# An attention and MLP kernel on one core: quad 0 turned at full width, its loads reordered, one A@V evacuated by two engines

## The chip, the cores and the metric

The kernel runs on 1 core of one Trainium2 chip. The metric is the device time of one execution in microseconds (us). An experiment gives several timed executions, each with the core's span and its mean granted TensorE clock, and one profile of one execution. All executions here count as "fast" (none is 1.5% above the fastest of its kernel).

Engines: PE is the TensorE matmul, PEld its weight load, DVE is VectorE, ACT ScalarE, POOL GpSimd, SP SyncE. The granted clock is the share of TensorE's full clock that the trace records; below, "warm" is the full clock (1.00 in the traces) and "cold" half of it (0.50).

## The reference

```python
# q, k, v: (8, 12, 448, 64) fp32; then an MLP over 3584 tokens, 768 -> 2048 -> 768
scores = np.matmul(q, k.transpose(0, 1, 3, 2)) / np.sqrt(64)
attn   = np.maximum(scores, 0.0) ** 2 / 448
x      = np.matmul(attn, v)                      # (..) -> (3584, 768)
h      = x @ w_in
g      = np.maximum(h, 0.0) + alpha * np.minimum(h, 0.0)
out    = g @ w_out
```

## The kernel before

Heads are handled four at a time, in a "quad"; there are 24 quads, three per batch. For each quad q and k are cast to bf16, turned (transposed) and multiplied; the scores get relu and square on ACT and DVE, then A@V follows and its result is scaled into `xT`, the MLP's input. Quad 0 is loaded as fp32 and cast on chip; quads 1 to 5 come by casting transfers that GpSimd issues. To keep these from taking bandwidth from quad 0, GpSimd first waits for the small load of alpha. The code is shortened; `...` and comments stand for what is left out.

```python
nc.scalar.dma_start(out=alpha_sb, in_=moe_alpha...)          # ahead of all
nc.sync.dma_start(out=raw[(0, "q")]..., in_=flat(0, "q"))
for js in (first, rest):
    nc.sync.dma_start(out=raw[(0, "k")][:, :, lo:hi]..., in_=...)
make_identity(nc, ident); make_identity(nc, ident_f)
cast[(1, "k")] = early_pool.tile([128, 2, NJ, D], BF16, tag="k", name="ke")
nc.gpsimd.tensor_copy(cast[(1, "k")][:KF, 0, 0, 0:1], alpha_sb[:, 0:1])   # the wait
nc.gpsimd.dma_start(out=cast[(1, "k")]..., in_=flat(1, "k"))
load_bf16(1, "q"); load_bf16(0, "v"); load_bf16(1, "v")
warm(15)                                    # dummy matmuls
nc.vector.tensor_copy(cast[(0, "q")][:, 0], raw[(0, "q")][:, 0])
nc.scalar.copy(cast[(0, "q")][:, 1], raw[(0, "q")][:, 1])
transpose(0, "q")
# ... k likewise, then scores(0, 0..2); the loop over quads 0 to 2:
            if j == 3 and not last:
                transpose(n + 1, "k")
            if j == 4 and not last:          # after this step's squares
                transpose(n + 1, "q")
                squares(keep=1)
# ... the turn itself, two 64-column matmuls for each j:
        for j in js:
            for s in range(2):
                nc.tensor.transpose(ps[64 * s:64 * s + 64, j], t[:, s, j], ident)
# ... the last A@V of batch 1 and its neighbours:
    ffn1(1, 0, range(0, 4)); ffn1(1, 1, range(0, 4))
    attnv(5)                                 # one tile, one ACT evacuation of 896
    feed(7, "v")()
    ffn1(1, 2, range(0, 4))
    for ff in range(3):
        ffn1(1, ff, range(4, KM))            # needs attnv(5)'s result
```

## Time and profile before

| | us |
|---|---|
| median of the first 3 executions | 391.43 |
| span of the profiled one | 390.1 |
| raw q of quad 0 lands | 4.61 |
| first scores | 6.66 |
| first MLP matmul | 22.22 |
| from there to the end | 367.86 |

The last four rows are read from starts and landings in the trace. They cut the span into four pieces, landing of q, landing to first scores, first scores to first MLP matmul, and the rest. The lines themselves stand in the prediction.

### The profile page before, as it was taken

What the parts mean: (1) busy time and instruction counts of PE and PEld (TensorE: products, weight loads), DVE (VectorE), ACT (ScalarE), POOL (GpSimd) and SP (SyncE); (2) the same over time, 40 slices, a digit from 0 to 9 for tenths busy, and PEclk for the clock granted to TensorE, in tenths of its full rate; (3) what the DMA queues carried; (4) which work ended last, traced back from release to release, by engine and by line L of the source; (5) the groups of instructions that cost most, each with busy time, mean ns of one, the idle gap of its engine ahead of it and who ended that gap; (6) DMA issues with size and microseconds to landing.
All of it is one profiled execution on the core that took longest, in us unless ns stands there. A gap on an engine that the chain in (4) does not pass through costs nothing.

```text
span 390.1 us, 7871 instructions
## 1 busy us (share of the span) xinstructions
PE 379.2 (97%) x3210; PEld 215.0 (55%) x3210; DVE 252.1 (65%) x335; ACT 215.6 (55%) x361; POOL 73.3 (19%) x88
## 2 busy tenths in 40 slices
PE   7699999999999999999999999999999999999996
PEld 4345556445665456645665456654566545655564
DVE  3976877587677757766674666777676376725411
ACT  5975767574556656654474645766565365624200
POOL 5664000061241014201231012311030000000000
PEclk9999999999999999999999999999999999999999
DMA  7999997893995528926494354947163220130033
GB/s 155 185 208 205 203 221 271 239 319 83 237 271 184 114 76 232 229 64 165 87 276 141 66 164 96 247 159 172 30 91 85 72 47 2 42 81 2 0 82 81
DMA packets 64755, 55.43 MB, mean 142 GB/s; under 512 B 35776, under 2 KB 60496, under 8 KB 64720
## 3 DMA queue, kind: packets, MB, share of 16 engines
q1 hardware_dynamic: 53472, 44.77, 44.2%
q0 software_dynamic: 10976, 9.96, 16.1%
q8 instruction: 25, 0.41, 0.4%
q10 hardware_dynamic: 272, 0.21, 0.2%
q14 instruction: 10, 0.08, 0.1%
HBM read 45.62 MB, written 11.01 MB: 145 GB/s over the span
## 4 chain that ended last, share of the span: by engine, by line
PE 94%; DMA 3%; ACT 1%; DVE 1%; issue 0%
PE hps L255 37%; PE ops L271 37%; PE avh L223 7%; PE sc L156 6%; PE sch L156 3%; DMA ke<-in_k_dram 2%; PE ops L294 1%; PE tps L131 1%; PE av L223 1%; DMA qraw<-in_q_dram 1%; ACT rl L185 1%; ACT xT L241 0%; DVE gT L263 0%; ACT rl L163 0%; DVE rl L165 0%
## 5 line engine op out<-in xcount | busy, mean ns | idle before, releaser
L255 PE MATMUL hps<-xT,w_in_sb 128*128 128x448 bf16 x768 | 149.3, 353 | 0.8 <-ACT xT L232 0.4
L271 PE MATMUL ops<-w_out_sb,gT 128*128 128x384 bf16 x864 | 145.8, 326 | 0.0
L263 DVE SCALAR_TENSOR_TENSOR gT<-neg,beta_sb,hps 128x448 bf16<-128x448 f32 x128 | 85.7, 679 | 61.1 <-ACT neg L262 60.2
L271 PEld LDWEIGHTS <-gT 128*128 128x128 bf16 x864 | 83.4, 98 | 61.2 <-issue 7.9
L255 PEld LDWEIGHTS <-w_in_sb 128*128 128x128 bf16 x768 | 74.0, 98 | 72.8 <-issue 5.9
L262 ACT ACTIVATE neg<-hps 128x448 f32<-128x448 f32 x128 | 69.0, 545 | 63.8 <-PE hps L255 63.7
L185 ACT ACTIVATE rl<-sc 128x896 bf16<-128x896 f32 x87 | 77.1, 923 | 44.4 <-PE sc L156 44.3
L196 DVE TENSOR_TENSOR at<-rl 128x1792 bf16<-128x1792 bf16 x80 | 85.5, 1112 | 2.1 <-ACT rl L185 0.9
L106 DVE COPY osb<-ops 128x384 f32<-128x384 f32 x30 | 16.7, 557 | 46.0 <-PE ops L271 46.0
L163 ACT ACTIVATE rl<-sch 128x448 bf16<-128x448 f32 x81 | 41.6, 550 | 4.6 <-PE sch L156 4.6
L106 POOL CAST kb<-kraw 128x896 bf16<-128x896 f32 x16 | 18.4, 1152 | 115.2 <-DMA kT<-kb 55.7
L156 PE MATMUL sc<-qT,kT 64*64 64x448 bf16 x456 | 35.9, 355 | 3.8 <-ACT rl L185 1.5
L223 PE MATMUL avh<-at,vb 64*64 64x448 bf16 x588 | 34.2, 350 | 0.0
L156 PEld LDWEIGHTS <-kT 64*64 64x64 bf16 x672 | 21.9, 106 | 20.1 <-issue 13.0
L104 ACT COPY osb<-ops 128x384 f32<-128x384 f32 x24 | 11.4, 475 | 36.0 <-PE ops L271 36.0
L223 PEld LDWEIGHTS <-vb 64*64 64x64 bf16 x672 | 25.6, 106 | 9.3 <-issue 4.9
L183 DVE TENSOR_SCALAR rl<-sc 128x896 bf16<-128x896 f32 x27 | 29.4, 1090 | 0.6 <-PE sc L156 0.6
L106 POOL CAST vb<-vraw 128x896 bf16<-128x896 f32 x16 | 16.8, 1050 | 36.5 <-PE avh L223 36.0
L156 PE MATMUL sch<-qT,kT 64*64 64x448 bf16 x216 | 22.5, 355 | 0.0
L106 POOL CAST qb<-qraw 128x896 bf16<-128x896 f32 x16 | 15.9, 991 | 32.3 <-DMA qT<-qb 32.3
L165 DVE TENSOR_SCALAR rl<-sch 128x448 bf16<-128x448 f32 x27 | 16.8, 622 | 2.6 <-ACT xT L239 0.8
L238 DVE TENSOR_SCALAR xT<-avh 128x448 bf16<-128x448 f32 x19 | 11.9, 625 | 7.7 <-PE avh L223 7.7
(55 smaller groups left out, 96.8 us busy)
## 6 DMA issues: line engine op xcount, KB each, us to landing
out_dram<-osb SPq DMA_DIRECT2D x54, 192.0 KB, 2.7
qraw<-in_q_dram SPq DMA_DIRECT2D x19, 448.0 KB, 5.4
kraw<-in_k_dram SPq DMA_DIRECT2D x18, 448.0 KB, 4.4
vraw<-in_v_dram SPq DMA_DIRECT2D x18, 448.0 KB, 6.3
w_out_sb<-in_moe_w_out_dram POOLq DMA_DIRECT2D x2, 1536.0 KB, 20.0
w_in_sb<-in_moe_w_in_dram POOLq DMA_DIRECT2D x8, 192.0 KB, 8.3
w_in_sb<-in_moe_w_in_dram POOLq DMA_DIRECT2D x4, 384.0 KB, 9.7
vb<-in_v_dram POOLq DMA_DIRECT2D x6, 224.0 KB, 9.7
```

Of the source, the lines that this page charges most:

```text
L106: eng.tensor_copy(o, i)
L156: nc.tensor.matmul(half[r][64 * c:64 * c + 64, :S], kT[n][64 * r:64 * r + 64, j, c, :], qT[n][64 * r:64 * r + 64, :, c, :], start=True, st ...
L163: nc.scalar.activation(rl[:, r], half[r][:, :S], ACTF.Relu)
L165: nc.vector.tensor_scalar(rl[:, r], half[r][:, :S], 0.0, None, ALU.max)
L183: nc.vector.tensor_scalar(rl, ps[:, :, :S], 0.0, None, ALU.max)
L185: nc.scalar.activation(rl, ps[:, :, :S], ACTF.Relu)
L196: nc.vector.tensor_tensor(a, t, t, ALU.mult)
L223: nc.tensor.matmul(half[r][64 * s:64 * s + 64, :S], vb[n][64 * r:64 * r + 64, s, j, :], a[64 * r:64 * r + 64, s], start=(j == 0), stop=(j ...
L255: nc.tensor.matmul(ps, w_in_sb[:, km // 2, km % 2, bass.ts(ff, 128)], xT[b][:, km // 2, km % 2, :], start=(km == 0), stop=(km == KM - 1))
L262: nc.scalar.activation(neg, ps, ACTF.Relu, scale=-1.0)
L263: nc.vector.scalar_tensor_tensor(gT[b // 2][:, ff, (b % 2) * S:(b % 2) * S + S], neg, beta_sb[:, ff:ff + 1], ps, ALU.mult, ALU.add)
L271: nc.tensor.matmul(ps, gT[sb][:, ff, bass.ts(c, 128)], w_out_sb[:, ff, bass.ts(hf, 384)], start=(ff == 0), stop=(ff == KF - 1))
```

## The change

It is meant to shorten the opening: fewer transposes for quad 0, nothing ahead of its load, casting transfers that start after a fixed delay instead of after alpha. One more edit lets two engines evacuate the last A@V of batch 1 side by side. A piece of dead code goes as well (not shown).

```diff
+        if n == 0:
+            t = t.rearrange("p j s d -> p j (s d)")
...
         for j in js:
+            if n == 0:
+                nc.tensor.transpose(ps[:, j], t[:, j], ident)
+                continue
             for s in range(2):
...
-    nc.scalar.dma_start(out=alpha_sb, in_=moe_alpha.rearrange("(kf p) -> kf p", p=128))
-        cast[(0, w)] = early_pool.tile([128, 2, NJ, D], BF16, tag=w, name=f"{w}e")
+        cast[(0, w)] = early_pool.tile([128, NJ, 2, D], BF16, tag=w, name=f"{w}e")
...                                          # after the three loads of quad 0:
+    nc.sync.dma_start(out=alpha_sb, in_=moe_alpha.rearrange("(kf p) -> kf p", p=128))
-    cast[(1, "k")] = early_pool.tile([128, 2, NJ, D], BF16, tag="k", name="ke")
-    nc.gpsimd.tensor_copy(cast[(1, "k")][:KF, 0, 0, 0:1], alpha_sb[:, 0:1])
-    nc.gpsimd.dma_start(out=cast[(1, "k")]..., in_=flat(1, "k"))
-    load_bf16(1, "q")
+    for w in "qk":
+        cast[(1, w)] = early_pool.tile([128, 2, NJ, D], BF16, tag=w, name=f"{w}e")
+        nc.gpsimd.memset(cast[(1, w)], 0.0)
+    for w in "kq":
+        nc.gpsimd.dma_start(out=cast[(1, w)]..., in_=flat(1, w))
-    nc.vector.tensor_copy(cast[(0, "q")][:, 0], raw[(0, "q")][:, 0])
-    nc.scalar.copy(cast[(0, "q")][:, 1], raw[(0, "q")][:, 1])
+    nc.vector.tensor_copy(cast[(0, "q")][:, :, 0], raw[(0, "q")][:, 0])
+    nc.scalar.copy(cast[(0, "q")][:, :, 1], raw[(0, "q")][:, 1])
...                                          # k likewise
-    attnv(5)
+    attnv(5, apart=True)
```

More of the change, by code (lines that the diff above doesn't have):

```diff
@@ L325, in f @@
             squares()
-            for n, j in order:
-                if n < n_pe:
-                    continue
-                if j == 0:
-                    if n + 2 < NQ:
-                        load(n + 2)
-                    if n + 1 < NQ:
-                        transpose(n + 1, "k")
-                        transpose(n + 1, "q")
-                if j == 4 and n > 2 * NG and n + 2 < NQ:
-                    for w in "kqv":
-                        to_bf16(n + 2, w, nc.gpsimd)
         return f
@@ L361 @@
                           in_=flat(0, "k")[:, :, lo * D:hi * D])
+    nc.sync.dma_start(out=alpha_sb, in_=moe_alpha.rearrange("(kf p) -> kf p", p=128))
     make_identity(nc, ident)
     make_identity(nc, ident_f)
-    cast[(1, "k")] = early_pool.tile([128, 2, NJ, D], BF16, tag="k", name="ke")
-    nc.gpsimd.tensor_copy(cast[(1, "k")][:KF, 0, 0, 0:1], alpha_sb[:, 0:1])
-    nc.gpsimd.dma_start(out=cast[(1, "k")].rearrange("p s j d -> p s (j d)"), in_=flat(1, "k"))
-    load_bf16(1, "q")
+    for w in "qk":
+        cast[(1, w)] = early_pool.tile([128, 2, NJ, D], BF16, tag=w, name=f"{w}e")
+        nc.gpsimd.memset(cast[(1, w)], 0.0)
+    for w in "kq":
+        nc.gpsimd.dma_start(out=cast[(1, w)].rearrange("p s j d -> p s (j d)"), in_=flat(1, w))
     load_bf16(0, "v")
@@ L371 @@
     warm(15)
-    nc.vector.tensor_copy(cast[(0, "q")][:, 0], raw[(0, "q")][:, 0])
-    nc.scalar.copy(cast[(0, "q")][:, 1], raw[(0, "q")][:, 1])
+    nc.vector.tensor_copy(cast[(0, "q")][:, :, 0], raw[(0, "q")][:, 0])
+    nc.scalar.copy(cast[(0, "q")][:, :, 1], raw[(0, "q")][:, 1])
     transpose(0, "q")
-    nc.scalar.copy(cast[(0, "k")][:, :, :3], raw[(0, "k")][:, :, :3])
+    nc.scalar.copy(cast[(0, "k")][:, :3].rearrange("p j s d -> p s j d"), raw[(0, "k")][:, :, :3])
     transpose(0, "k", first, nc.scalar)
     warm(2)
-    nc.vector.tensor_copy(cast[(0, "k")][:, :, 3:], raw[(0, "k")][:, :, 3:])
+    nc.vector.tensor_copy(cast[(0, "k")][:, 3:].rearrange("p j s d -> p s j d"), raw[(0, "k")][:, :, 3:])
     scores(0, 0)
```

## The prediction

> **What bounds the kernel now.** I began with the page of the profiled execution, whose span is 390.1 us (the timed runs have a median of 391.43). Its first part, and the sums by stretch that I asked for next, say where a gain can lie at all. In the stretches the columns are the stretch in us, its length, then busy time and instruction count of PE, PEld, DVE, ACT and POOL, the granted clock, the DMA share and GB/s.
>
> ```profile
> PE 379.2 (97%) x3210; PEld 215.0 (55%) x3210; DVE 252.1 (65%) x335; ACT 215.6 (55%) x361; POOL 73.3 (19%) x88
> ...
> 4.20:8.00 3.80, 2.75 (x45) 1.48 (x43) 1.89 (x4) 2.42 (x5) 2.83 (x4) 1.00 0.90 164
> 8.00:12.00 4.00, 2.29 (x44) 1.21 (x44) 3.68 (x8) 4.00 (x7) 3.69 (x6) 1.00 1.11 155
> 12.00:16.00 4.00, 2.71 (x52) 1.76 (x54) 3.79 (x6) 3.62 (x7) 1.56 (x4) 1.00 1.21 188
> 16.00:22.20 6.20, 4.71 (x92) 2.62 (x87) 6.00 (x9) 5.84 (x10) 4.22 (x7) 1.00 1.23 199
> 22.20:30.00 7.80, 7.57 (x61) 3.50 (x61) 5.55 (x9) 4.57 (x8) 4.65 (x7) 1.00 1.14 210
> 30.00:72.00 42.00, 42.00 (x409) 23.20 (x410) 31.69 (x45) 26.91 (x41) 4.47 (x7) 1.00 1.10 221
> 72.00:75.00 3.00, 2.84 (x33) 1.29 (x26) 0.00 (x0) 1.27 (x2) 0.00 (x0) 1.00 0.92 257
> 75.00:380.00 305.00, 304.96 (x2427) 173.18 (x2426) 197.95 (x255) 165.16 (x285) 50.58 (x48) 1.00 0.51 128
> ```
>
> From 22.2 us to 380 us the PE is the bound: it idles 0.23 us in 22.2 to 30, nothing in 30 to 72, 0.16 in 72 to 75 and 0.04 in the other 305. The change does not touch the matmuls there, so it cannot shorten this long middle; it can only let it start earlier, or close the 0.16 us hole at 74. The tail is untouched too. In 8 to 22.2 us the bound is another: VectorE is busy 3.68 + 3.79 + 6.00 = 13.47 of 14.2 us and ScalarE 4.00 + 3.62 + 5.84 = 13.46, with relu and squares of the first three quads. So all waits together leave about 0.73 us on each of them, and that is the ceiling for whatever earlier transfers can give. Only the stretch before 8 us has a real dependency chain. The chain of waits in order of time shows it:
>
> ```profile
> 0.74 3.87 DMA qraw<-in_q_dram
> 4.63 0.44 DVE qe L372
> 5.12 0.99 PE tps L131 x20
> 6.13 0.49 ACT kT L104
> 6.66 0.57 PE sc L156 x8
> ...
> 7.50 0.64 DVE rl L165
> 8.31 7.40 DMA ke<-in_k_dram
> 15.76 0.58 PE tps L131 x14
> ```
>
> Load of quad 0, cast, 20 transposes, one evacuation, first scores. Then comes the transfer of quad 2's k, issued at 8.31 and landing at 15.7. It is long because it queues behind the earlier casting transfers: the DMA share is 0.9 to 1.2 throughout, so this queue runs at its rate from about 6.5 us on, and an earlier start moves all its landings.
>
> [...] (1) [...] 14 transposes of 128x64 take 0.58 us (8.82 us in the timeline), and less one 0.22 us latency that is 28 ns each, 55 ns for a pair. [...] (2) [...] The 448-element cast of q takes 426 ns and an 896-element one 620[...]. (3) [...] (4) [...] Here it is about 1.5: issued at 4.03, and the DMA share goes from 1 to 8 tenths between 5.0 and 5.5.
>
> **Part by part.** *Full-width turn of quad 0.* Removes 14 of 28 transposes (q 14 to 7, k 6 to 3, then 8 to 4). By point (1), 7 full turns at an estimated 55 ns equal 7 pairs at 55 ns: 0. It would be worse if a full 128-column weight load didn't hide behind its matmul[...]. The VectorE cast writes with a stride. [...] ScalarE's half ends at 5.20 and gates anyway[...]. I put this part at +0.05 us (0 to +0.2) on the first scores and all that follows.
>
> *Memsets in place of the wait for alpha.* GpSimd now idles 1.92 us for alpha and issues the first casting transfer at 4.03:
>
> ```profile
> 1.43 0.19 POOL masks.py:199 TENSOR_SCALAR_AFFINE_SELECT ident_f<-ident_f 16x16 f32<-16x16 f32 x1
> 3.54 0.18 POOL L366 CAST ke<-alpha_sb 16x1 bf16<-16x1 f32 x1 [1.92 <-DMA alpha_sb<-in_moe_alpha_dram]
> 4.03 0.84 POOL L367 DMA_DIRECT2D ke<-in_k_dram  x1 [0.31 <-POOL ke L366]
> ```
>
> A GpSimd memset takes 0.20 us for 128 elements and 0.10 for one, 0.8 ns per element, so 896 elements are an estimated 0.8 us; two end at 1.62 + 1.6 = 3.2. With the same 0.31 us gap the first issue is at about 3.55, 0.45 us earlier, and so are all casting landings. The raw transfers of quad 0 are mostly through by 5.0, where the first cast packets would now come, so they lose little.
>
> What does this buy? Quad 1's k lands at 8.08 and is not waited for; quad 2's k is, at 15.76:
>
> ```profile
> 15.76 0.58 PE L131 MATMUL tps<-ident,ke 128*64 128x128 bf16 x14 [0.58 <-DMA ke<-in_k_dram]
> ...
> 16.71 0.92 ACT L185 ACTIVATE rl<-sc 128x896 bf16<-128x896 f32 x1 [0.36 <-PE sc L156]
> ...
> 17.21 0.62 DVE L106 COPY qT<-tps 128x896 bf16<-128x896 bf16 x1 [0.20 <-PE tps L131]
> ```
>
> Of the 0.58 us only what starved the bound engines counts: ScalarE idles 0.36 and VectorE 0.20 behind it. With k at 15.3, VectorE still finishes a square at 16.47 before it can evacuate the turn, so I take its 0.20 as the gain, -0.2 us with an estimated spread of 0 to -0.4.
>
> *alpha behind quad 0.* It goes from ScalarE's queue to the end of SyncE's; landing around 6, it is needed at 7.69. 0 us.
>
> *A@V of quad 5 in two tiles.* Now one ScalarE evacuation of 896 elements follows it:
>
> ```profile
> 73.10 0.92 ACT L241 ACTIVATE xT<-av 128x896 bf16<-128x896 f32 x1 [3.42 <-PE av L223]
> ...
> 74.07 3.00 PE L255 MATMUL hps<-xT,w_in_sb 128*128 128x448 bf16 x15 [0.16 <-ACT xT L241]
> ```
>
> With two tiles VectorE takes one half (0.62 us, as at 21.81) and ScalarE the other (about 0.59, as at 15.76), side by side, ready at 73.75. PE has other matmuls until 73.91, so the hole of 0.16 us closes, and no more can be had: -0.15. VectorE's cast of vb at 70.97 now stands behind this evacuation in its program order and moves to about 73.7, but its next work is at 75.22. Both score buffers are free by then, as the last score was at 67.0. The lines removed from the group helper serve only quads from 6 on; the helper is called for quads up to 5, so they never run.
>
> Sum: +0.05 - 0.2 + 0 - 0.15 = -0.3. The fourth rival below, at about one chance in four for another -0.5, adds -0.1: -0.4, and 391.43 - 0.4 is 391.0.
>
> **Rivals.** First: *the earlier casting transfers gain nothing*, because VectorE and ScalarE are over 90% busy from 8 to 22 us and every wait removed turns up at the next one. The 13.47 of 14.2 us speak for it; the 0.36 and 0.20 us directly behind the transfer speak against it. Then -0.1 in all, 391.3. Second: *the opening chain gets slower*, because strided casts and full-width weight loads cost more than the pairs did; +0.2 to +0.4, and the total lands at 391.3 to 391.7. The 98 ns weight load of 128 columns against 106 of 64 speaks against it. Third: *the memsets take longer*, nearer the 1.0 to 1.15 us of GpSimd's casts of 896 elements; then the first issue is at 4.2, later than now, and the transfer waits grow by 0.2: 391.4. Fourth: *the whole 0.73 us of waits in 8 to 22 us goes away*, since two engines waiting for each other can both be eased at once: 390.4.
>
> **Range and chances.** The best sum I can defend is -0.73 - 0.16, about 390.5, a little lower if the opening gains too; the worst +0.4, 391.8. Three runs of before spread over 0.4 us. I give 390.2 to 391.7. Two per cent is 7.8 us and no part reaches a tenth of that, so within 2% is almost sure.
>
> **What would show it right or wrong.** In the changed trace: the first casting issue at 3.4 to 3.7 us and quad 2's k landing near 15.3; 7 transposes for q in about 0.55 us; the first scores at 6.6 to 6.8; the first MLP matmul at 22.0 instead of 22.22; no wait before the matmuls at 74; PE's busy time unchanged from there. The prediction is wrong if memsets take well over 1 us, if the first score comes later than 7.0, if the DMA queue slows quad 0's own loads, or if a new wait appears between 22 and 72 us because weights arrive in another order.

Cut from the recorded text, where marked, is what no trace or run of this case shows. Of point (1) the 28 and 55 ns are from the trace of before. The 55 ns of a full turn is the estimate; the traces bear it out: in before, matmuls of 448 columns start 0.19 us apart (15 take 3.00 us, one alone 0.35), which is 54 ns for 128 columns, and in q_first_early_turn seven full turns took 0.55 us. Point (4) is about the time from the issue of a casting transfer to its first bytes: the first packet of that queue starts at 5.57 us in the trace of before, 1.5 us after the start of the issuing instruction (4.03) and 0.7 us after its end (4.87). The DMA share is 0.19 from 5.0 to 5.5 and 0.87 from 5.5 to 6.0, so the rise is one slice later than the prediction read it.

## The result, and the profile after

Six executions took 390.68, 390.70, 391.05, 392.49, 392.56 and 392.59 us, median 391.77, against a median of 391.36 (391.17 to 391.85) for six of the kernel before. The ratio was 1.0007, 95% interval 0.9983 to 1.003: the same. (Ratios are the mean time of one kernel's fast runs over that of the other's of the same rounds, so not quite the ratio of the medians.)

The median hides two groups with nothing between 391.05 and 392.49. The slow three have a mean granted clock of 0.993 to 0.996, the quick three 0.999 or 1.0. The profiled execution, span 390.7, is a slow one. Here are its sums by stretch, with the same columns as in the prediction (stretch, length, busy time of PE, PEld, DVE, ACT and POOL, clock, DMA share, GB/s), and below them four stretches of 3.41 us. (The clock of 1.00 in the first line is not a reading of all of it: this trace has no clock record before 6.55 us.)

```profile
4.20:8.00 3.80, 3.19 (x31) 1.82 (x29) 1.98 (x4) 2.31 (x5) 2.28 (x4) 1.00 0.96 163
8.00:12.00 4.00, 2.22 (x44) 1.21 (x44) 3.68 (x8) 4.00 (x6) 3.72 (x6) 1.00 1.17 160
12.00:16.00 4.00, 3.31 (x40) 2.00 (x44) 3.79 (x5) 3.08 (x5) 2.39 (x5) 0.67 1.21 183
16.00:22.20 6.20, 5.09 (x96) 2.76 (x92) 5.16 (x8) 5.52 (x9) 3.50 (x6) 0.94 1.22 193
...
72.00:75.00 3.00, 3.00 (x37) 1.40 (x36) 1.00 (x2) 0.54 (x1) 0.00 (x0) 1.00 0.91 229
```

```profile
6.55:9.97 3.41, 2.73 (x51) 1.60 (x53) 2.36 (x6) 2.92 (x6) 1.69 (x3) 1.00 1.16 163
9.97:13.38 3.41, 1.51 (x30) 0.67 (x25) 3.31 (x5) 3.04 (x6) 3.41 (x6) 1.00 1.16 163
13.38:16.79 3.41, 3.34 (x36) 1.77 (x37) 2.97 (x4) 2.19 (x5) 1.37 (x3) 0.50 1.23 196
16.80:20.21 3.41, 2.54 (x52) 1.34 (x49) 2.72 (x5) 3.41 (x6) 1.88 (x3) 1.00 1.20 185
```

The third line of the second block is the loss: from 13.38 to 16.79 us the granted clock is 0.50. PE is busy for 3.34 us of it and gets only 36 matmuls done (a second, undisturbed execution has 68 in 13.21 to 16.62), ACT and DVE wait for it (ACT 1.23 us for an A@V, DVE 0.84 for a turn), and the first MLP matmul comes at 23.13 us in place of 22.22 (the undisturbed execution has 21.78; 22.0 was predicted). In the line above it, the window before the fall, PE is busy for only 1.51 us. Of its idle time 1.33 us is one wait: DVE finishes a square before it evacuates the turned q.

```profile
10.38 1.08 DVE L201 TENSOR_TENSOR at<-rl 128x1792 bf16<-128x1792 bf16 x1
11.38 0.61 DVE L106 COPY qT<-tps 128x896 bf16<-128x896 bf16 x1
12.05 0.57 PE L161 MATMUL sc<-qT,kT 64*64 64x448 bf16 x8 [1.33 <-DVE qT L106]
```

GpSimd did what was forecast: two memsets of 0.83 us and the first casting issue at 3.48. The last line is the issue of quad 2's k.

```profile
1.56 0.83 POOL L360 MEMSET qe<- 128x896 bf16 x1
2.34 0.83 POOL L360 MEMSET ke<- 128x896 bf16 x1
3.48 0.84 POOL L362 DMA_DIRECT2D ke<-in_k_dram  x1 [0.31 <-POOL ke L360]
...
8.28 0.72 POOL L100 DMA_DIRECT2D ke<-in_k_dram  x1 [1.80 <-DVE rl L170]
```

The hole at 74 us is closed. In the timeline the matmuls now run on, and DVE and ACT evacuate half a tile each:

```profile
73.89 3.78 PE L260 MATMUL hps<-xT,w_in_sb 128*128 128x448 bf16 x19
...
74.00 0.62 DVE L243 TENSOR_SCALAR xT<-av 128x448 bf16<-128x448 f32 x1 [2.04 <-PE av L228]
74.04 0.54 ACT L244 ACTIVATE xT<-av 128x448 bf16<-128x448 f32 x1 [3.45 <-PE av L228]
```

### The profile page after: what moved, and what is told of

Its sections match the earlier page's. It is cut to its first block, busy times and chain, and to the rows that moved or that the text cites. A ratio compares the mean times of both kernels' runs of the same rounds, so it can differ in the third digit from the quotient of the medians.

```text
span 390.7 us, 7846 instructions
## 1 busy us (share of the span) xinstructions
PE 381.0 (98%) x3196; PEld 215.8 (55%) x3196; DVE 252.2 (65%) x336; ACT 215.2 (55%) x361; POOL 74.7 (19%) x89
## 4 chain that ended last, share of the span: by engine, by line
PE 95%; ACT 2%; DVE 1%; DMA 1%; issue 0%
PE hps L260 37%; PE ops L276 37%; PE avh L228 8%; PE sc L161 6%; PE sch L161 3%; PE ops L299 1%; ACT rl L190 1%; PE av L228 1%; PE tps L136 1%; DMA qraw<-in_q_dram 1%; DVE at L201 0%; PE tps L133 0%; DVE gT L268 0%; ACT rl L168 0%; DVE qe L366 0%
## 5 line engine op out<-in xcount | busy, mean ns | idle before, releaser
L106 POOL CAST kb<-kraw 128x896 bf16<-128x896 f32 x16 | 20.4, 1274 | 116.9 <-DMA kT<-kb 54.0
L228 PE MATMUL avh<-at,vb 64*64 64x448 bf16 x588 | 35.5, 360 | 0.0
L106 POOL CAST vb<-vraw 128x896 bf16<-128x896 f32 x16 | 15.8, 989 | 38.2 <-PE avh L228 37.7
L106 POOL CAST qb<-qraw 128x896 bf16<-128x896 f32 x16 | 14.9, 934 | 29.7 <-DMA qT<-qb 29.7
```

The costliest lines, as they stand in the source:

```text
L106: eng.tensor_copy(o, i)
L228: nc.tensor.matmul(half[r][64 * s:64 * s + 64, :S], vb[n][64 * r:64 * r + 64, s, j, :], a[64 * r:64 * r + 64, s], start=(j == 0), stop=(j ...
```

## The experiments

Twelve kernels ran, in three groups of four; the kernels of a group share eleven executions of the kernel before on the same chip. "no_turn" and later names are labels. The medians:

| kernel | executions | median | range | over 392 us | ratio to before (95%) |
|---|---|---|---|---|---|
| after_again | 6 | 391.16 | 390.77 to 391.86 | 0 | 0.9984 (0.9961 to 1.0006) |
| no_turn | 6 | 390.79 | 390.50 to 392.31 | 1 | 0.9978 (0.9954 to 1.0003) |
| av_only | 8 | 391.39 | 391.00 to 393.06 | 2 | 0.9983 (0.9959 to 1.0007) |
| turn_only | 6 | 391.26 | 391.15 to 392.34 | 2 | 0.9992 (0.9969 to 1.0015) |
| alpha_first | 6 | 391.23 | 390.95 to 392.64 | 1 | 0.9988 (0.9965 to 1.0012) |
| late_cast | 6 | 393.27 | 392.21 to 395.27 | 6 | 1.0041 (1.0012 to 1.0069) |
| q_first | 6 | 390.78 | 390.39 to 390.89 | 0 | 0.9967 (0.9944 to 0.9990) |
| q_first_turn | 6 | 391.05 | 390.72 to 391.23 | 0 | 0.9975 (0.9954 to 0.9996) |
| before_q_first | 6 | 391.65 | 391.04 to 393.99 | 2 | 0.9998 (0.9966 to 1.0030) |
| q_first_early | 6 | 390.91 | 390.67 to 391.29 | 0 | 0.9969 (0.9946 to 0.9992) |
| q_first_early_turn | 6 | 390.91 | 390.52 to 391.17 | 0 | 0.9967 (0.9944 to 0.9991) |
| q_first0_early | 6 | 390.91 | 390.36 to 392.27 | 1 | 0.9972 (0.9946 to 0.9997) |

The kernel before had a median of 391.48, 391.61 and 392.05 in the three groups, and 13 of all its 39 executions were over 392 us.

The intervals are wider than most effects, because of these slow executions. So I read the parts of the change from the traces, by the cut into four pieces. Each row is one execution; the columns are times in us, the last tells when the clock was first at full rate and whether it fell again. Before the first record the clock was half, as the matmuls show: in after_again, turns of 128 columns start 107 ns apart before 6.38 us (seven take 0.91 us), and 55 ns apart in the warm opening of q_first_early_turn (seven take 0.55).

| trace | q lands | to first scores | to first MLP matmul | to the end | full clock from |
|---|---|---|---|---|---|
| before | 4.61 | 2.05 | 15.56 | 367.86 | 4.16 |
| after | 4.06 | 2.58 | 16.49 | 367.56 | 6.55, half 13.38 to 16.79 |
| after_again | 4.10 | 2.58 | 15.10 | 367.57 | 6.38 |
| no_turn | 3.92 | 2.05 | 15.10 | 367.56 | 4.69 |
| av_only | 4.32 | 2.04 | 17.27 | 367.58 | 4.04, half 10.86 to 17.69 |
| turn_only | 4.24 | 2.29 | 15.10 | 367.88 | 5.50 |
| alpha_first | 4.24 | 2.49 | 15.09 | 367.63 | 6.41 |
| late_cast | 3.95 | 2.48 | 19.42 | 367.57 | 6.07, half 9.48 to 19.72 |
| q_first | 3.99 | 2.01 | 15.41 | 367.59 | 4.15 |
| q_first_turn | 4.01 | 2.58 | 15.04 | 367.60 | 6.42 |
| before_q_first | 4.36 | 2.36 | 14.94 | 368.40 | 5.89 |
| q_first_early | 4.04 | 2.48 | 15.12 | 367.58 | 6.92 |
| q_first_early_turn | 3.98 | 2.08 | 15.02 | 367.57 | 4.54 |
| q_first0_early | 4.10 | 2.45 | 16.26 | 367.59 | 5.81, half 9.22 to 12.64 |

**after_again: the changed kernel, unedited.**

> The changed kernel once more, unedited. Theory A (a clock lottery): its executions fall into two groups, those with a mean granted clock of 0.999 or 1.0 at 390.6 to 391.1 us, and those with about 0.993 to 0.996 at 392.4 to 392.7, because the PE was put at half clock for one stretch of 3.41 us between 10 and 17 us; the kernel before stays in one group, 391.1 to 391.9. Theory B (the lottery is in both kernels, six runs were too few): the kernel before also shows executions with a clock below 0.999 at 393.0 or so. Theory C (ordinary spread): times don't go with the clock.

All six were below 392 (390.77 to 391.86, clocks 0.998 and 0.999), while 4 of the 11 executions of the kernel before were over 392 (392.76 to 393.43). Theory B holds: the slow group belongs to both kernels, and six executions had been too few. Theory C falls in part: of those four, two have a clock of 0.991 and 0.994, but two show 1.0. In the trace of after the clock record starts at 6.55 us, at 1.00, though its turns before that start about 105 ns apart; so its mean of 0.996 leaves out the cold opening (3.41 us at half clock in the 384 us from 6.55 on give just that). Whether that explains these two is open.

**no_turn: quad 0 in halves again, all else as changed.** The five `+` lines of the turn are taken out and casts and tiles of quad 0 are as before.

> The changed kernel with quad 0 turned in halves again as before (casts and transposes as before); loads, memsets and the two-tile A@V stay. If the full-width turn is what makes the half-clock stretch likely, all executions have clock 0.999 or more and lie at 390.5 to 390.9 us. If it is the earlier start or the loads, about half of them still lie at 392.5. Where the clock is full, the cast of q on VectorE takes 0.43 us again (0.62 in the changed kernel), so first scores are up to 0.1 us earlier.

One of six was slow (392.31, clock 0.996), so the half clock comes without the turn too, as it did in the kernel before; one of six is too few to tell whether the turn makes it likelier. The other five have a median of 390.66. The expectation of a 0.43 us cast was too simple: here DVE's half took 0.57, and in the halved kernels 0.39 to 0.57, against 0.62 in all five traces with the full-width turn.

**av_only: the kernel before with the A@V edit alone.**

```diff
-    attnv(5)
+    attnv(5, apart=True)
```

> The kernel before with the last A@V of batch 1 in two PSUM tiles and nothing else. My prediction had this close a PE hole of 0.16 us: -0.15 us against the kernel before, 391.2 where that is 391.36; no half-clock stretch in either. If the evacuation was hidden anyway: 0.0.

The two slow executions spoil the times, but the last piece of the trace is untouched by them: 367.58, against 367.86 and 367.88 in the traces of before and turn_only, and 367.56 to 367.63 in the other ten traces with this edit. It buys 0.29 us, nearly twice what was expected. (The remaining trace without it, before_q_first, has 368.40; there PE also waited 0.34 us for a piece of w_in.) Six executions below 392 have a median of 391.25, against 391.23 for the seven of before on that chip, so the times alone would not have shown it.

**turn_only: the kernel before with the full-width turn alone.**

> The kernel before with quad 0 turned at full width and nothing else. My prediction had +0.05 us (0 to +0.2). If the full-width turn makes the half-clock stretch likely, a part of its executions lie at 393 us with a clock under 0.999; if not, all lie at 391.2 to 391.7.

Four executions lie at 391.15 to 391.29, two at 392.09 and 392.34. Before's seven below 392 on that chip are at 391.14 to 391.59. No cost shows at this resolution. Neither branch of the expectation came as written: the two slow executions are at 392 and not 393, with recorded clocks of 0.999 and 1.0. The trace's 2.29 is between the others as its clock rose in the middle of the opening, at 5.50.

**alpha_first: no_turn with alpha loaded first again.**

```diff
+    nc.scalar.dma_start(out=alpha_sb, ...)     # ahead of quad 0, as before
-    nc.sync.dma_start(out=alpha_sb, ...)       # behind quad 0
```

> The no_turn kernel with one line moved back: alpha is loaded first and from ScalarE's queue, as in the kernel before; the memsets stay. Theory A (the small alpha load ahead of quad 0 delays quad 0's own load): raw q lands at 4.2 to 4.6 us in place of 3.9 to 4.1; first scores 2.05 us later (6.3 to 6.6 in place of 5.97); from first scores to first MLP matmul 15.1 us and from there to the end 367.57 us, both unchanged; undisturbed executions at 390.85 to 391.1 against 390.5 to 390.6 of no_turn. Rival B (raw q's landing is chance or follows from the memsets): raw q at 3.9 to 4.1 and undisturbed executions at 390.5 to 390.6.

Raw q lands at 4.24. The five traces with alpha first have 4.24 to 4.61 (mean 4.35), the nine with alpha behind quad 0 have 3.92 to 4.10 (mean 4.02); the groups don't touch, and this pair differs in that one line. Moving alpha buys 0.3 us up to q's landing. The five executions below 392 have a median of 391.14 (390.85 to 391.1 was expected). From issue to landing of raw q in alpha_first, then in no_turn (the views of this tile, us, min/median/max):

```profile
DMA to landing us min/median/max: 3.5/3.5/3.5
```

```profile
DMA to landing us min/median/max: 3.2/3.2/3.2
```

First scores were expected at 2.05 after the landing; it was 2.49, since this execution had a cold clock until 6.41. That the place of this one line costs the time is shown. How is not. In the trace alpha does not run ahead of raw q but beside it: SyncE issues q at 0.74 and ScalarE alpha at 0.74. And the line moves something else too: behind alpha's issue ACT's table load starts at 1.23 us in place of 0.73, and ends at 2.51. From 2.0 to 2.5 us the DMA engines are busy for 0.29 to 0.36 of the time in the five traces with alpha first and for 0.48 to 0.77 in the nine others. Here are alpha_first and then no_turn; the last two columns are the DMA share and GB/s:

```profile
2.00:2.50 0.50, 0.50 (x4) 0.37 (x3) 0.00 (x0) 0.50 (x1) 0.50 (x2) 1.00 0.36 93
```

```profile
2.00:2.50 0.50, 0.50 (x4) 0.37 (x3) 0.00 (x0) 0.02 (x1) 0.50 (x2) 1.00 0.70 161
```

No run parts alpha's own bytes from the later table load, so that rival stays open.

**late_cast: no_turn with each memset issued twice.**

```diff
-        nc.gpsimd.memset(cast[(1, w)], 0.0)
+        for _ in range(2):
+            nc.gpsimd.memset(cast[(1, w)], 0.0)
```

> The no_turn kernel with each memset issued twice, so that the casting transfers start about 1.6 us later, at 5.1 us in place of 3.48. My prediction had quad 2's k gate the stretch, so an earlier start buys time and this later one would cost 0.3 to 1.2 us. Theory A (the kernel's one trace had an unusually late quad 2, at 15.7 against 13.1 to 14.3 in five others): k of quad 2 lands at about 14.7, still before it is needed at about 15, first scores to first MLP matmul stays at 15.1 us, undisturbed executions within 0.1 us of 390.5 to 390.7.

My theory fell. The first casting issue came at 5.46, and all six executions were over 392; even the fastest, with a recorded clock of 1.0, took 392.21. Not quad 2 but quad 1 was late (quad 2's k landed at 15.60, 14.7 was expected, and PE did not wait for it). The PE timeline:

```profile
9.54 0.96 PE L131 MATMUL tps<-ident,ke 128*64 128x128 bf16 x14 [0.87 <-DMA ke<-in_k_dram]
10.43 0.59 PE L156 MATMUL sc<-qT,kT 64*64 64x448 bf16 x4
12.26 0.96 PE L131 MATMUL tps<-ident,qe 128*64 128x128 bf16 x14 [1.24 <-DMA qe<-in_q_dram]
```

PE waits 0.87 us for quad 1's k and 1.24 us for its q. In the changed kernel's trace q landed at 9.51 and cost no wait on the path. So there is a deadline: issues from 2.70 to 3.69 us leave 15.1 us unchanged (q_first_early 2.70, no_turn 3.48, turn_only 3.69), and 5.46 is past it. And the half clock follows a stretch of 3.41 us in which PE is busy for only 1.88, as the windows show:

```profile
6.07:9.48 3.41, 1.88 (x27) 0.76 (x25) 2.36 (x6) 2.92 (x5) 3.41 (x6) 1.00 0.80 104
9.48:12.90 3.41, 2.12 (x30) 1.52 (x32) 1.86 (x3) 1.27 (x2) 2.75 (x5) 0.50 1.08 149
12.90:16.30 3.40, 2.76 (x30) 0.98 (x30) 2.61 (x4) 2.53 (x4) 1.90 (x4) 0.50 1.26 202
16.31:19.72 3.41, 3.41 (x44) 1.99 (x38) 2.37 (x3) 2.19 (x5) 1.73 (x4) 0.50 1.23 199
```

Three windows of 3.41 us at half clock: the piece up to the first MLP matmul took 19.42 us.

**q_first: no_turn with the next quad's q turned ahead of the squares.**

```diff
+            if j == 4 and not last:
+                transpose(n + 1, "q")
             if j == 6 and last:
                 squares()
...
             if j == 4 and not last:
-                transpose(n + 1, "q")
                 squares(keep=1)
```

> The no_turn kernel with the turn of the next quad's q put ahead of the squares in step 4, so that VectorE evacuates it about 1 us sooner and PE's idle stretch of 1.33 us near 11 us shrinks to about 0.4. Theory A [...]: [...] no execution falls to 392 us or more for that reason, and first scores to first MLP matmul falls from 15.1 to 14.7 to 15.0. Rival: VectorE was the bound and the same square only comes later, 15.1 stays; the lottery goes on.

All six executions lie within 0.5 us, 390.39 to 390.89, with the lowest median of all (no_turn's, on another chip, is 0.01 us higher), and PE does more in the place of the weak window:

```profile
10.98:14.39 3.41, 2.37 (x40) 1.26 (x40) 3.31 (x4) 3.41 (x6) 2.47 (x5) 1.00 1.22 192
```

PE is busy for 2.37 us of it, against 1.51 in the changed kernel and 1.69 in the nearest window of the kernel before (10.99 to 14.40). The second half of the expectation missed: to the first MLP matmul it took 15.41 us, not 14.7 to 15.0. The wait of 1.33 us shrank to 0.22, but DVE now idled 0.37 us for the turn of quad 1's q, which landed at 9.53:

```profile
10.20 0.62 DVE L106 COPY qT<-tps 128x896 bf16<-128x896 bf16 x1 [0.37 <-PE tps L131]
10.88 0.38 PE L156 MATMUL sc<-qT,kT 64*64 64x448 bf16 x4 [0.22 <-DVE qT L106]
```

These six executions are steadier; the undisturbed path is not shorter.

**q_first_turn: the changed kernel with the same edit.**

> The changed kernel with the same edit as q_first. Against q_first it tells the cost of the full-width turn alone: by the casts (0.62 against 0.43 us on VectorE, of which 0.06 got through) +0.1 us with a warm clock from landing of raw q to first scores (2.05 becomes 2.15), and 2.58 where the clock is still half. Rival: it costs nothing with a warm clock.

The median is 391.05 against 390.78. The trace has a cold opening, 2.58 us, like after and after_again; cold openings in halves take 2.48 or 2.49 where the clock rose at 6.07 or later (alpha_first, late_cast, q_first_early). Full width costs 0.1 us there.

**before_q_first: the kernel before with this order alone.**

> The kernel before with one edit: in step 4 the turn of the next quad's q stands ahead of the squares. Theory A (the half-clock lottery belongs to the schedule that both kernels share, not to the change): of its executions fewer than the 8 of 28 of the kernel before are over 392 us, at most one of six[...]; its undisturbed time stays 391.0 to 391.3. Rival (the change's other parts removed the lottery in q_first): one third of its executions stay above 392.

Two of six were over 392 (392.42, recorded clock 1.0; 393.99, clock 0.991), where I had expected at most one. So the order alone does not end the slow executions under the old opening.

**q_first_early: q_first with one memset in place of two.**

```diff
-        nc.gpsimd.memset(cast[(1, w)], 0.0)
+        if w == "k":
+            nc.gpsimd.memset(cast[(1, w)], 0.0)
```

> q_first with one memset in place of two, so that the casting transfers start about 0.8 us earlier (2.7 in place of 3.48). In q_first VectorE idled 0.37 us for quad 1's q, which landed at 9.53. Theory A: q of quad 1 lands at 8.7 to 9.0, that idle goes, first scores to first MLP matmul falls from 15.41 to 15.1 or less, time 390.2 to 390.6, no execution over 392. Rival (the earlier casts take bandwidth from quad 0's own loads): raw q still lands at 4.0, but k's second part lands later than 6.0 and first scores come later; time 390.8 or more.

Casting starts at 2.70, quad 1's q lands at 8.74, raw q still at 4.04, and the middle piece is 15.12 us, as expected. The time is not below q_first's: 390.67 to 391.29, where 390.2 to 390.6 was expected. No gain from the earlier start. The rival shows in part: the second part of quad 0's k lands at 5.91 here, and at 6.12 and 7.44 in the next two kernels, which start their casts as early; the eleven traces with later casts have 5.43 to 6.04.

**q_first_early_turn: the same with the full-width turn.**

> The same with quad 0 turned at full width, the second pair that tells the cost of this part alone. From q_first and q_first_turn (medians 390.78 and 391.05): 0.2 to 0.3 us slower than q_first_early. In a trace with a warm clock from 4.8 us on: raw q's landing to first scores 2.10 to 2.2 against 2.01 to 2.05 in halves. Rival: with a warm clock it costs nothing, and the medians are within 0.1.

The medians are equal at 390.91, so this pair shows no cost, the one before it 0.27 us. But this trace is the one with full width and a warm clock from the start: 2.08 us from landing to first scores, against 2.01 to 2.05 in halves. The PE lines of the opening, first this trace, warm, then after_again, cold:

```profile
4.77 0.55 PE L133 MATMUL tps<-ident,qe 128*128 128x128 bf16 x7 [0.29 <-DVE qe L367]
5.16 0.33 PE L133 MATMUL tps<-ident,ke 128*128 128x128 bf16 x3
```

```profile
4.89 0.91 PE L133 MATMUL tps<-ident,qe 128*128 128x128 bf16 x7 [0.40 <-DVE qe L366]
5.59 0.53 PE L133 MATMUL tps<-ident,ke 128*128 128x128 bf16 x3
```

Seven turns take 0.55 us warm and 0.91 cold. In halves, no_turn has for q (its clock rose at 4.69, 0.12 us into this line):

```profile
4.57 0.62 PE L131 MATMUL tps<-ident,qe 128*64 128x128 bf16 x14
```

**q_first0_early: the new order for quad 1 alone.**

> q_first_early with the new order for the turn of quad 1 only; quad 2's q stands behind the squares again. Theory A: quad 1's turn is what fills the weak window, so no execution is over 392 us; quad 2's early turn only made VectorE wait, so first scores to first MLP matmul is 15.0 to 15.1 and the time 390.2 to 390.5, the best of all. Rival: no difference to q_first_early within 0.1 us.

One of six was slow (392.27), and it is the profiled one: at 9.22 the clock fell to 0.50 for one window (to 12.64), after a window from 5.81 in which PE was busy for 2.17 of 3.41 us. In that window DVE and then PE waited for the second part of quad 0's k, which landed 2 us later than in q_first (7.44 against 5.43):

```profile
7.46 0.43 DVE L368 CAST ke<-kraw 128x512 bf16<-128x512 f32 x1 [1.11 <-DMA kraw<-in_k_dram]
```

So this slow execution says little about the order of the turns; it fits what the rival of q_first_early warned of. The other five took 390.36 to 391.28. The kernel is not better than q_first.

## Why the prediction was right or wrong

**The total.** Predicted were 391.0 and within 2%. The first six executions had a median of 391.77, just above the range of 390.2 to 391.7 (which left out the prediction's own worst sum, 391.8), and the six of after_again 391.16, inside it; the twelve together have 391.16, and the 39 of the kernel before 391.59. Within 2% was right beyond doubt. That the sum of -0.4 agrees with those medians is luck: three of its four terms were mis-sized, and one cause was not in it.

**What the four terms measured.**

- *Full-width turn: right.* Predicted +0.05 (0 to +0.2). Measured +0.03 to +0.07 with a warm clock (2.08 against 2.01 to 2.05), +0.1 with a cold one; the two pairs of medians say 0.27 and 0. The reasons hold too. A pair of 64-column matmuls already cost about as much as one of 128: seven turns took 0.55 us, as estimated, and seven pairs 0.58 (before, at 8.82). The strided cast took 0.62 us on DVE in all five traces, where the contiguous one took 0.39 to 0.57 (why it is slower is not shown), and ACT's 0.565 hid all but 0.055 of it.
- *Earlier casting transfers: mis-sized, -0.2 became 0.* The first issue came at 3.48 (3.55 predicted). The step that failed is that an earlier start moves all landings. Quad 2's k takes a tile from a pool of two, so it must wait until quad 0's k is done with. GpSimd waits there for DVE, 1.28 us before and 1.80 after, and issues at 8.31 and 8.28: the 0.55 us gained at the first issue don't reach this one. And the wait that was to shrink was a feature of one trace. There quad 2's k landed at 15.71; in the twelve other traces whose casts started by 3.81 us it landed at 12.68 to 14.28, three of those with the old loads (turn_only 13.39, av_only 13.61, before_q_first 14.14). From first scores to first MLP matmul, turn_only with the old loads takes 15.10, exactly as no_turn and after_again do, while the trace of before took 15.56. Why that one transfer was late is open; that it queued behind the earlier ones, as I had read it, was not shown. My first rival, that ACT and DVE are the bound in this stretch and earlier casts gain nothing, came nearest: the earlier casts gained nothing. That those two engines are the reason was not tested.
- *alpha behind quad 0: mis-sized, 0 became about -0.3.* I only asked whether alpha would still be in time. It was (6.23 in the changed trace, needed at 7.67). I did not ask what its load, issued at the same moment as raw q's, does to raw q: with alpha last, q lands 0.34 us earlier on average, and that landing starts the chain of the whole opening. Whether alpha's bytes or the later table load of ACT held q up is open.
- *A@V in two tiles: right mechanism, mis-sized, -0.15 became -0.29.* I read the size of the hole from PE's idle time, 0.16 us, and that was the wrong reading. The record of one of these matmuls lasts 0.35 us (0.352 in the median of before), but in the changed trace they start 0.19 us apart (19 take 3.78 us, less one of 0.35, over 18 steps). Four from 72.98 at 0.19 us each make room for a fifth at 73.74, and the next started at 74.07: the hole between starts was 0.33 us. The idle column counts from the end of the last record, at 73.91, and so shows 0.16.

For an undisturbed execution with a warm opening these give -0.34 + 0.05 + 0 - 0.29, about -0.58. The times show less: below 392 us the 26 executions of the kernel before have a median of 391.41 and the nine of the changed one 391.06, and the fastest are 391.03 and 390.68, 0.35 in both. Both traces of the changed kernel had a cold opening (0.5 us) and that of before a warm one; whether this accounts for the difference can't be told from three traces.

**What was not in it: the clock.** The prediction took the granted clock of 1.00 in every stretch of before's trace as given, and none of its rivals mentions it. In four traces it fell to half for one to three stretches of 3.41 us. In three of them the middle piece was 1.2 to 2.2 us longer than 15.1, more than all parts of the change together, and in late_cast 4.3; in all but after, a late transfer has its part in this. Of before's 39 executions 13 are over 392 us, of the changed kernel's 12 three; nothing shows that the change made it more or less likely, and the first session's 3 of 6 against 0 of 6 may well be chance. I predicted first scores at 6.6 to 6.8 and they came at 6.64, but only because an earlier q (0.55 us) and a cold opening (0.5 us) cancelled: a number can be right with both its terms wrong.

**What sets it off.** In these four traces the half clock lasted 3.41 us (after, 13.38 to 16.79; q_first0_early, 9.22 to 12.64), 6.83 (av_only, 10.86 to 17.69) or 10.24 (late_cast, 9.48 to 19.72), and it began 3.41 or 6.83 us after the clock had risen: one to three times 3.41 us, each time. In the window of 3.41 us just ahead of the fall PE was busy for 1.51 us (after), 1.88 (late_cast), 1.94 (av_only) and 2.17 (q_first0_early). That alone does not part the windows: before kept its clock after 1.69 us, after_again after 1.73 and alpha_first after 1.74. Nor does the count of matmuls: 43 in the window of av_only, 32 in that of before. PE had waited ahead of each of the four falls (below), but what parts these windows from the others is not shown.

PE's work can be missing for two reasons. In after, PE waits near 11 us for DVE's evacuation of the turned q behind a square, 1.33 us; the trace of before has the same wait, 1.27 us, and kept its clock, with its windows at other places (7.58 to 10.99 and 10.99 to 14.40, against 9.97 to 13.38). In the other three traces that lost the clock, PE waited for a late transfer: av_only 0.89 us for quad 1's q (landed at 10.27), late_cast 0.87 us for quad 1's k ahead of the fall (and 1.24 for its q after it), q_first0_early by way of DVE, which waited 1.11 us for quad 0's k. The wait in av_only:

```profile
10.31 0.58 PE L131 MATMUL tps<-ident,qe 128*64 128x128 bf16 x14 [0.89 <-DMA qe<-in_q_dram]
```

The new order fills the first spot: in q_first the wait is 0.22 us in place of 1.33, and PE is busy for 2.37 us of the window in its place. It does not bring late transfers in earlier.

None of 24 executions of q_first, q_first_turn, q_first_early and q_first_early_turn was over 392, against 5 of 24 of the changed kernel, no_turn and alpha_first, which also have the memsets, and 4 of 14 of av_only and turn_only with the old opening. That the order helps together with the new opening is thus supported, by small counts and not within the same rounds. With the old opening it was not enough (2 of 6, neither profiled), and why is open, as are slow executions with a recorded clock of 1.0.

**The best version.** q_first, which is the changed kernel without its full-width turn and with the turn of the next q ahead of the squares, ran at 390.78 against 391.61 for the kernel before on the same chip: a ratio of 0.9967 (0.9944 to 0.9990), 0.3% faster and with the smallest spread of all; q_first_early_turn has the same ratio on another chip. Against the changed kernel there is no run of the same rounds; q_first_turn, which differs from the changed kernel by the order alone, had 0.9975.

## What to carry to other kernels

Take a wait in one trace as a sample: before a forecast rests on a transfer's landing time, see whether it is the same in a second execution, and whether its own issue moves at all. Read a hole in PE's work from the starts of the matmuls, not from its idle time, which here showed 0.16 us of 0.33. And where the engines wait for each other in turn, look at PE's idle stretches as well: four traces here fell to half clock after windows of 3.41 us with 1.24 to 1.90 us of idle PE, and their middle piece was 1.2 to 4.3 us longer (three others kept their clock after 1.67 to 1.72). An order that left PE less idle there, 0.22 us of a wait in place of 1.33, went with none of 24 executions over 392 us, where the parts that shortened the path gained 0.3 us each.
